# A complex linear recurrence moved from TensorE's cumulative sums to VectorE's scans, and the whole kernel issued in a hand-made order

## The chip, the cores and the metric

The kernel runs on one core of a Trainium2 chip. The metric is the device time of the launch in microseconds (us). Before the change it is 260.15 us (median of 4 runs, 259.61 to 260.87).

The engines are named as in the profile: PE is TensorE (PEld its weight loads), DVE is VectorE, ACT is ScalarE, POOL is GpSimd, SP the queue that issues most DMA transfers. "Span" is the time from the first to the last instruction in the trace; the launch time lies about 2 us above it (260.2 against 258.2 before the change).

## The reference, cut to what matters

Sequence length L = 2048, width 512, 512 complex states, hidden width F = 1792, all in bf16.

```python
xn = layernorm(x)                                    # [1, 2048, 512]
# A: diagonal complex state-space recurrence
Lam_bar = exp(dt * Lam)                              # one complex number per state, |Lam_bar| < 1
Bu = xn @ B_bar.T                                    # complex, [2048, 512]
h[t] = Lam_bar * h[t-1] + Bu[t]                      # for t in range(2048)
A = 2 * real(h @ C.T) + xn * Dskip
# B: gated feed-forward
B = (silu(xn @ w1) * (xn @ w3)) @ w2
out = x + A + B
```

The feed-forward is most of the arithmetic. The two schemes differ in how they do the recurrence.

## The kernel before

Time is cut into 16 chunks of 128 steps, with time on the partitions. Inside a chunk the recurrence is a cumulative sum: the inputs are multiplied by `Lam_bar**-t`, summed over time by a matmul with a triangular matrix, the last state of the chunk before is added by a second matmul, and the result is multiplied by `Lam_bar**t`. The states then have time on the partitions and have to be transposed by DMA for the output matmul.

```python
def ssm_chunk(cl, xnT, h_prev):
    ...                                          # bu_re, bu_im: 4 matmuls each, evicted to bu16 by ACT
    ca = bu16 * einv_re_b                        # 128x1024, DVE
    cb = bu16 * einv_im_b
    zp[:, 0, :] = ca[:, 0, :] - cb[:, 1, :]      # 128x512
    zp[:, 1, :] = ca[:, 1, :] + cb[:, 0, :]
    for ri in range(2):
        hp = ps_mm.tile([P, PS], FP32, name="mm_ps")
        nc.tensor.matmul(out=hp, lhsT=u_caus, rhs=zp[:, ri, :], start=True, stop=(h_prev is None))      # L329
        if h_prev is not None:
            nc.tensor.matmul(out=hp, lhsT=sel, rhs=h_prev[:, ri, :], start=False, stop=True)            # L331
    ...                                          # evicted by ACT, the same four DVE operations with e_re_b, e_im_b
    nc.sync.dma_start_transpose(out=hT16, in_=h16.rearrange("p a b -> p (a b)"))
    return h16, hT16

def glu_up(xnT, hgT):
    for f in range(NFT):                         # 14 steps for each of 4 blocks of 512 rows
        ...                                      # g_ps, u_ps: 4 matmuls each
        nc.scalar.activation(out=th16, in_=g_ps, func=ACT.Tanh, scale=0.5)
        nc.scalar.activation(out=u16, in_=u_ps, func=ACT.Copy, scale=0.5)
        nc.vector.scalar_tensor_tensor(out=th16, in0=th16, scalar=1.0, in1=g_ps, op0=ALU.add, op1=ALU.mult)
        nc.vector.tensor_tensor(out=hgT[:, f, :], in0=th16, in1=u16, op=ALU.mult)
```

A scheduler chooses the order of the instructions on each engine. The layer norm's 1/sqrt is a chain of some ten small DVE operations per chunk in the first block, and the normalised rows are transposed by PE (64 matmuls against an identity).

## Time and profile before

| | before |
|---|---|
| time, median | 260.15 us |
| span of the profiled run, granted TensorE clock | 258.2 us, 1.000 |
| busy: PE, DVE, ACT | 88%, 71%, 49% |
| first gate matmul starts | 24.11 us |
| last output matmul ends | 254.6 us |
| PE waits after the first gate matmul, sum in the view of waits | about 4.5 us |

The view of waits lists who waited for whom: total us, number of times, longest. These are the largest PE entries of the kernel before:

```profile
PE y_ps L286 <- DVE rstd_all L258: 21.1, 2, 18.0
PE gu_ps L297 <- ACT u_339 L302: 1.5, 1, 1.5
PE gu_ps L297 <- ACT u_307 L302: 1.5, 1, 1.5
PE gu_ps L297 <- ACT u_355 L302: 0.7, 1, 0.7
```

The first line is the start: PE waits 18.0 us for the first rstd and once more 3.1 us. Everything else is small. The timeline gives the first gate matmuls and the last output matmuls (start, us, engine, line, operation, how many); four matmuls of 512 columns take 1.87 us at the start, and 1.03 from 27.41 us on:

```profile
24.11 1.87 PE L293 MATMUL gu_ps<-xnT,w_sb 128*128 128x512 bf16 x4 [0.69 <-ACT xnT L287]
...
251.43 3.19 PE L362 MATMUL y_ps<-w_sb,hgT 128*128 128x512 bf16 x14
```

The table of busy time by stretch says that PE is the limit from 45 us on (columns: stretch, its length, busy us and instructions of PE, PEld, DVE, ACT, POOL, then granted clock, DMA share, GB/s):

```profile
28.00:45.00 17.00, 13.21 (x89) 7.14 (x89) 13.48 (x36) 16.62 (x27) 0.00 (x0) 1.00 0.72 158
45.00:62.00 17.00, 16.63 (x104) 8.62 (x105) 16.89 (x44) 12.22 (x22) 0.00 (x0) 1.00 0.01 2
...
150.00:200.00 50.00, 49.73 (x224) 22.28 (x228) 33.47 (x70) 23.02 (x40) 0.00 (x0) 1.00 0.13 30
```

From 150 to 200 us PE is busy 49.73 of 50. PE also counts as busy when it works at half pace (the stretch from 24.10 to 27.40 us is 3.29 of 3.30 us busy with 8 gate matmuls, which start 0.41 us apart on average), so the pitch has to be read too: 22 output matmuls take 4.75 us in the timeline, 0.216 us each. The groups that the change removes or replaces (busy us, mean ns of one; the mean of an L329 matmul is 378 ns, longer than the pitch of 216):

```profile
L329 PE MATMUL mm_ps<-zp,u_caus 128*128 128x512 bf16 x32 | 12.1, 378 | 0.4 <-DVE zp L324 0.2
L337 DVE TENSOR_TENSOR ca<-h16s,e_tab 128x1024 bf16<-128x1024 bf16 x16 | 11.1, 691 | 4.8 <-ACT h16s L335 4.5
```

### The profile page before, as it was taken

How to read it: one execution, taken by the hardware profiler on the slowest of the kernel's cores; microseconds unless marked ns; L12 is line 12 of the kernel's file. 1: busy time of each engine (PE TensorE's matmuls, PEld its weight loads, DVE VectorE, ACT ScalarE, POOL GpSimd, SP SyncE). 2: the span in 40 equal slices, each digit the busy share in tenths (PEclk: the TensorE clock that was granted, in tenths of full speed). 3: DMA queues.
4: the chain of work that ended last, by engine and by line, in shares of the span. 5: the costliest groups of instructions: out<-in, count | busy, mean ns of one | idle time of the engine just before them, and what ended most of it. 6: DMA issues, size and time to landing. Idle time of an engine off the chain costs nothing. (4 is left out here: it accounts for less than half of the span.)

```text
span 258.2 us, 3287 instructions
## 1 busy us (share of the span) xinstructions
PE 227.1 (88%) x1096; PEld 104.7 (41%) x1118; DVE 184.4 (71%) x496; ACT 125.4 (49%) x216; POOL 1.6 (1%) x11
## 2 busy tenths in 40 slices
PE   0014976999999999999999999999999999999994
PEld 0012443455434445444444544444444444444441
DVE  1749887999999739999635399996343899984331
ACT  0614899677733108777400477776100677764000
POOL 2000000000000000000000000000000000000000
PEclk9999999999999999999999999999999999999999
DMA  5999982000122300222201002222010022220000
GB/s 156 155 361 381 349 161 25 1 1 3 23 55 44 83 22 20 41 43 41 42 20 42 22 0 41 42 43 41 0 41 23 20 41 41 43 44 0 20 34 27
DMA packets 33873, 16.73 MB, mean 65 GB/s; under 512 B 23360, under 2 KB 33856, under 8 KB 33856
## 3 DMA queue, kind: packets, MB, share of 16 engines
q1 hardware_dynamic: 31696, 16.00, 23.7%
q10 hardware_dynamic: 2160, 0.53, 2.0%
q8 instruction: 8, 0.13, 0.2%
q14 instruction: 9, 0.07, 0.1%
HBM read 9.18 MB, written 2.10 MB: 44 GB/s over the span
## 5 line engine op out<-in xcount | busy, mean ns | idle before, releaser
L297 PE MATMUL gu_ps<-xnT,w_sb 128*128 128x512 bf16 x222 | 59.4, 382 | 4.1 <-ACT u_339 L302 1.5
L293 PE MATMUL gu_ps<-xnT,w_sb 128*128 128x512 bf16 x218 | 58.5, 383 | 0.9 <-ACT xnT L287 0.7
L362 PE MATMUL y_ps<-w_sb,hgT 128*128 128x512 bf16 x218 | 50.8, 379 | 0.3
L297 PEld LDWEIGHTS <-w_sb 128*128 128x128 bf16 x224 | 21.9, 98 | 31.4 <-issue 9.1
L293 PEld LDWEIGHTS <-w_sb 128*128 128x128 bf16 x224 | 22.1, 99 | 27.5 <-issue 2.1
L362 PEld LDWEIGHTS <-hgT 128*128 128x128 bf16 x224 | 21.9, 98 | 26.4
L287 ACT ACTIVATE xnT<-y_ps 128x512 bf16<-128x512 bf16 x16 | 8.6, 604 | 41.2 <-PE y_ps L286 41.2
L314 PE MATMUL mm_ps<-bbar_im,xnT 128*128 128x512 bf16 x64 | 16.4, 379 | 0.1
L286 PE MATMUL y_ps<-ident,xn_170 128*128 128x128 bf16 x4 | 0.6, 308 | 18.0 <-DVE rstd_all L258 18.0
L310 PE MATMUL mm_ps<-bbar_re,xnT 128*128 128x512 bf16 x61 | 16.3, 378 | 0.1
L337 DVE TENSOR_TENSOR ca<-h16s,e_tab 128x1024 bf16<-128x1024 bf16 x16 | 11.1, 691 | 4.8 <-ACT h16s L335 4.5
L334 ACT ACTIVATE h16s<-mm_ps 128x512 bf16<-128x512 f32 x16 | 9.5, 596 | 9.8 <-PE mm_ps L331 9.4
L329 PE MATMUL mm_ps<-zp,u_caus 128*128 128x512 bf16 x32 | 12.1, 378 | 0.4 <-DVE zp L324 0.2
L339 DVE TENSOR_TENSOR cb<-h16s,e_tab 128x1024 bf16<-128x1024 bf16 x16 | 10.9, 684 | 0.0
L268 DVE BATCH_NORM_STATS2 stats<-x_blk 128x6 f32<-128x512 bf16 x12 | 8.0, 674 | 3.6 <-DMA x_blk<-in_A_x_dram 3.6
L317 ACT ACTIVATE bu_2120<-mm_ps 128x512 bf16<-128x512 f32 x1 | 0.6, 597 | 19.2 <-PE mm_ps L310 19.2
L335 ACT ACTIVATE h16s<-mm_ps 128x512 bf16<-128x512 f32 x16 | 9.5, 595 | 0.0
L314 PEld LDWEIGHTS <-xnT 128*128 128x128 bf16 x64 | 6.3, 98 | 7.6
L310 PEld LDWEIGHTS <-xnT 128*128 128x128 bf16 x64 | 6.1, 97 | 6.6 <-issue 0.7
L286 PEld LDWEIGHTS <-xn_170 128*128 128x128 bf16 x4 | 0.3, 132 | 18.0 <-DVE rstd_all L258 18.0
L324 DVE TENSOR_TENSOR zp<-ca,cb 128x512 bf16<-128x512 bf16 x16 | 6.7, 416 | 0.0
L325 DVE TENSOR_TENSOR zp<-ca,cb 128x512 bf16<-128x512 bf16 x16 | 6.7, 416 | 0.0
(599 smaller groups left out, 364.6 us busy)
## 6 DMA issues: line engine op xcount, KB each, us to landing
w_sb<-in_B_w_dram SPq DMA_DIRECT2D x4, 640.0 KB, 9.6
x_blk<-in_A_x_dram SPq DMA_DIRECT2D x4, 512.0 KB, 8.9
w_sb<-in_B_w_dram SPq DMA_DIRECT2D x1, 1792.0 KB, 12.5
w_sb<-in_B_w_dram SPq DMA_DIRECT2D x2, 512.0 KB, 7.6
b_re_sb<-in_A_B_re_dram SPq DMA_DIRECT2D x1, 512.0 KB, 8.8
b_im_sb<-in_A_B_im_dram SPq DMA_DIRECT2D x1, 512.0 KB, 8.8
ldt_row<-in_A_log_dt_dram ACTq DMA_DIRECT2D x1, 128.0 KB, 6.0
lre_row<-in_A_Lambda_re_dram ACTq DMA_DIRECT2D x1, 128.0 KB, 6.9
```

The costliest lines, as they stand in the source:

```text
L268: nc.vector.bn_stats(out=stats[:, cl, :], in_=xb[:, cl, :])
L287: nc.scalar.activation(out=xnT[:, :, cl * P:(cl + 1) * P], in_=pxt, func=ACT.Copy)
L293: nc.tensor.matmul(out=g_ps, lhsT=w1_sb[:, dt, f * P:(f + 1) * P], rhs=xnT[:, dt, :], start=(dt == 0), stop=(dt == NDT - 1))
L297: nc.tensor.matmul(out=u_ps, lhsT=w3_sb[:, dt, f * P:(f + 1) * P], rhs=xnT[:, dt, :], start=(dt == 0), stop=(dt == NDT - 1))
L310: nc.tensor.matmul(out=bu_re, lhsT=xnT[:, dt, tsl], rhs=bbar_re[:, dt, :], start=(dt == 0), stop=(dt == NDT - 1))
L314: nc.tensor.matmul(out=bu_im, lhsT=xnT[:, dt, tsl], rhs=bbar_im[:, dt, :], start=(dt == 0), stop=(dt == NDT - 1))
L329: nc.tensor.matmul(out=hp, lhsT=u_caus, rhs=zp[:, ri, :], start=True, stop=(h_prev is None))
L334: nc.scalar.activation(out=h16s[:, 0, :], in_=h_ps[0], func=ACT.Copy)
L335: nc.scalar.activation(out=h16s[:, 1, :], in_=h_ps[1], func=ACT.Copy)
L337: nc.vector.tensor_tensor(out=ca2, in0=h16s, in1=e_re_b, op=ALU.mult)
L339: nc.vector.tensor_tensor(out=cb2, in0=h16s, in1=e_im_b, op=ALU.mult)
L362: nc.tensor.matmul(out=y_ps, lhsT=hgT[:, f, tsl], rhs=w2_sb[:, f, :], start=(k == 0), stop=(k == nmm - 1))
```

## The change

The intent is to take the recurrence off TensorE. The states lie on the partitions and time runs along the free axis. The inputs are rotated by `exp(-i*theta*t)`, which leaves a decay by the real number `rho` per state, so the complex recurrence becomes two real ones; each is one scan instruction on VectorE over 512 steps. The result is rotated back, and it already has the layout that the output matmul needs. The 32 cumulative-sum matmuls, the 30 carry matmuls, 64 small setup matmuls and the 16 DMA transposes of states go. The gate uses one Silu eviction and one bf16 product instead of three steps. Transposes of the normalised rows go to DMA for blocks 1 to 3.

The scheduler is switched off. The program emits everything in a written order; a small helper (`Filler`) keeps a queue of VectorE tasks with costs in us, and each PE step calls `bg.fill(budget)`, which emits as many tasks as the budget pays for. The core of the diff:

```diff
+    ctx.enter_context(tc.manual_schedule())
...
+        def pre(pt):                       # rotate the input of one tile of 128 states
+            ...                            # tiles are made; u is the input, st keeps v and g
+            nc.vector.tensor_tensor(out=p1, in0=u, in1=tabq[:, pt, 0:2, :], op=ALU.mult)
+            nc.vector.tensor_tensor(out=p2, in0=u, in1=tabq[:, pt, 2:3, :].to_broadcast([P, 2, TBLK]), op=ALU.mult)
+            nc.vector.tensor_tensor(out=v, in0=p1, in1=p2[:, ::-1, :], op=ALU.subtract)
+        def scan(pt, ri):
+            init = 0.0 if b == 0 else h_blk[b - 1][:, pt, ri, TBLK - 1:TBLK]
+            nc.vector.tensor_tensor_scan(out=st["g", pt][:, ri, :], data0=rho[:, pt:pt + 1].to_broadcast([P, TBLK]),
+                                         data1=st["v", pt][:, ri, :], initial=init, op0=ALU.mult, op1=ALU.add)
+        def post(pt): ...                  # two products and a difference like pre, into h_blk
+        for pt in range(NPT):
+            bg.add(2.0, lambda pt=pt: pre(pt))
+            bg.add(1.1, lambda pt=pt: scan(pt, 0))
+            bg.add(1.1, lambda pt=pt: scan(pt, 1))
+            bg.add(2.0, lambda pt=pt: post(pt), ("ssm", b))
...
+    def y(b):                              # output stage, 4 groups of 128 rows; y_ps has 2 buffers
+        for cl in range(CPB):
+            ...                            # 22 matmuls into y_ps
+            pend.append((cl, y_ps))
+            bg.fill(4.0)                   # (100.0 behind the very last group)
+            while len(pend) > 1:
+                finish()                   # o = y_ps + residual on DVE: this frees the y_ps buffer
...
+    bg.add(0.2, params_w)                  # block 0: tables, and the layer norm of block 1
+    for i in range(NPT + 1):
+        if i < NPT:
+            bg.add(1.9, lambda pt=i: table_angles(pt))
+        for t in ln1a[i:i + 1]:            # one statistics task of block 1 per state tile
+            bg.add(*t)
+        if i >= 1:
+            bg.add(2.1, lambda pt=i - 1: table_q(pt))
+    for t in ln1b:                         # normalise block 1, transpose it by DMA
+        bg.add(*t, ("ln", 1))
+    ...
+    gate = glu(0); bg.flush(("ln", 1)); gate()
+    ssm_tasks(0); bu(0)
+    ...
+    gate = glu(1); gate(); ssm_tasks(1); res_tasks(1); bu(1)
+    fin = y(0)
```

## The prediction

> **What bounds the kernel now.** TensorE, from its first real matmul to the end. The timeline has the first gate matmul at 24.1 us and the last one ending at 254.65; in the stage table PE is 97 to 99% busy from 45 us on, at full granted clock. The longest PE wait in the waits view is the 18.0 us before the first transpose, then 3.1 us for the second half of the layer norm: VectorE had queued later work (and waits for DMA) between the pieces of the first rstd. From 28 to 45 us PE is only 13.2 of 17 us busy, with ScalarE 16.6 busy. VectorE is 71% busy, ScalarE 49%.
>
> Pitch from the timeline: 22 output matmuls take 4.75 us (0.216 each[...]); a gate/up group of 8 takes 1.77.
>
> **Removed from PE.** 32 causal-sum and 30 carry matmuls: 62 x 0.216 = 13.4 us. 64 setup matmuls of 128 columns at 0.056: 3.6, plus about 1 of waiting among them. 48 of 64 layer-norm transposes (now DMA): 2.7. All of this is on the critical path: about 20 us. The ScalarE-bound patch before 45 us cost about 3.8; part comes back (below).
>
> **Moved earlier.** x block 0 arrives as four 128 KB pieces on two queues instead of 512 KB (first statistics at 5.5 us), rstd is Ln and Exp on ScalarE in strict order, weights start with 256 columns. Sum: data 4, two statistics 1.6, Ln/Exp 0.6, apply and transposes 1.4, twice in part: first gate matmul near 10.5 us, 13.5 earlier. It still runs about 3.5 us at half pace, as the first ones do before (4 in 1.87).
>
> **Added.** VectorE: 16 x (six 128x1024 products at 0.60 pitch + two scans). A scan has no duration in this trace[...]. That is 5.8 per state tile, 93 us in all; gates fall from 0.94 to 0.34 (56x: 19), norm 18, residual 9, outputs 10, tables 16: 165 us. Per gate/up step VectorE has about 1.55 us against PE's 1.77, so it keeps up, with little slack.
>
> **New PE time.** 56 steps x 1.77 = 99, 128 input matmuls 27.7, 352 output matmuls 76: 203. Start 10.5 + 203 + half-pace 1.7 = 215, + stalls: ScalarE in block 0 (28 evictions and 12 table sines fill about as long as PE's 24.5) and xnT of block 1, which waits for tables and four DMA transposes (a 256 KB one took 3.1): together 3; later 1.5. Last addition, output DMA and end 3.6 as now: span 223. Reported time lies 2 us above span before, so 225; some of these overlap, so I say 223.
>
> **Predicted: 223 us, 217 to 233.** Faster by over 2%: 0.97; within 2%: 0.02; slower: 0.01.
>
> **What shows it.** First gate matmul at 9 to 12 us; PE about 97% busy from then, output matmuls still 0.216 pitch; scans near 1.1 us; VectorE 75 to 80% of the span; PE waits in block 0 (ScalarE, xnT of block 1) of 2 to 5 us, few later; no PE wait on hidden states at the output matmuls.
>
> **What would make it wrong.** Scans or the reversed-half subtraction taking twice my estimate: VectorE would exceed 200 us and PE would wait on PSUM buffers, toward 235 to 245. GpSimd's chain of small operations holding ScalarE's first sines, which sit in front of evictions. First weights landing late (640 KB took 9.6 us before). Transposed loads of B late for block 0's input matmuls. [...]

The scan's duration, 1.1 us, goes into the forecast of VectorE's work. That sum came to 165 us and contains it: 16 x (6 x 0.60 + 2 x 1.1) is the 93, of which the 32 scans are 35, and the 1.55 us per gate/up step rests on it too. No trace showed a scan before the change, so the 1.1 is the author's estimate with no measurement behind it. The sum of the time, 10.5 + 203 + 1.7 + 3 + 1.5 + 3.6 = 223, contains no scan; 2 was added for the launch and 2 taken off for overlap. The 4 us for the first data is an estimate as well; the first statistics began at 3.4 us after the change.

## The result, and the profile after

The changed kernel takes 237.07 us (median of 4 runs, 236.85 to 237.39). The ratio to before is 0.911 (95% interval 0.909 to 0.913). Ratios here are the mean time of one kernel's runs over that of the other's of the same rounds, so they are not quite the ratio of the medians quoted. It is 23 us faster where 37 were predicted, and 4 us above the upper end of the range.

| | before | after |
|---|---|---|
| time, median | 260.15 us | 237.07 us |
| span, granted TensorE clock | 258.2 us, 1.000 | 234.7 us, 0.975 |
| first gate matmul starts | 24.11 us | 10.03 us |
| last output matmul ends | 254.6 us | 230.9 us |
| busy: PE, DVE, ACT | 88%, 71%, 49% | 90%, 74%, 41% |

The start came as predicted, and the tail is about the same as before (3.8 us behind the last output matmul, 3.6 before). What differs lies between. The PE entries of the view of waits, after:

```profile
PE y_ps L201 <- DVE xn L181: 8.2, 2, 6.3
PE y_ps L428 <- DVE o L421: 4.6, 2, 2.6
PE gu_ps L363 <- DMA xnT<-xn: 4.5, 1, 4.5
PE gu_ps L363 <- ACT g_439 L368: 1.0, 1, 1.0
PE gu_ps L363 <- ACT g_259 L368: 0.6, 1, 0.6
PE bu_ps L311 <- ACT u L313: 0.5, 1, 0.5
PE gu_ps L363 <- ACT g_360 L368: 0.3, 1, 0.3
```

The first line is the start (6.3 us instead of 18.0). The next two are new, long waits in the middle of the kernel: two at the output matmuls for the addition `o`, one at the gate matmuls for the transposed block 1. The timeline of PE shows where:

```profile
10.03 3.62 PE L363 MATMUL gu_ps<-xnT,w_sb 128*128 128x256 bf16 x16
...
51.46 10.91 PE L363 MATMUL gu_ps<-xnT,w_sb 128*128 128x512 bf16 x41 [4.52 <-DMA xnT<-xn]
...
96.44 4.87 PE L428 MATMUL y_ps<-w_sb,hgT 128*128 128x512 bf16 x14 [2.56 <-DVE o L421]
...
150.39 4.87 PE L428 MATMUL y_ps<-w_sb,hgT 128*128 128x512 bf16 x13 [2.04 <-DVE o L421]
```

Undisturbed, 14 output matmuls take 3.19 us; the groups after the two waits take 4.87 (one matmul record of the second is missing). The clock column of the table by stage explains it. The stages are, in order: gate/up of block 0; input matmuls of block 0 and the wait; gate/up of block 1; input matmuls of block 1, undisturbed; output of block 0; gate/up of block 2, undisturbed; output of block 1; output of block 2, undisturbed.

```profile
10.03:39.20 29.17, 27.20 (x130) 13.52 (x131) 19.60 (x46) 22.65 (x45) 6.83 (x26) 1.00 0.63 173
39.20:51.46 12.26, 7.17 (x33) 3.06 (x32) 11.91 (x25) 6.41 (x12) 1.35 (x2) 1.00 0.22 43
51.46:77.31 25.85, 25.75 (x110) 11.32 (x113) 19.79 (x34) 16.12 (x27) 0.00 (x0) 0.93 0.37 87
77.31:84.22 6.91, 6.86 (x32) 3.14 (x32) 5.91 (x8) 4.78 (x8) 0.00 (x0) 1.00 0.00 0
84.22:107.62 23.40, 20.74 (x88) 9.03 (x88) 19.83 (x32) 0.60 (x1) 1.26 (x2) 0.93 0.16 40
107.62:131.79 24.17, 24.07 (x111) 10.98 (x112) 22.30 (x38) 16.12 (x27) 0.00 (x0) 1.00 0.02 7
...
138.70:161.57 22.87, 20.78 (x88) 9.02 (x88) 20.72 (x28) 0.60 (x1) 0.00 (x0) 0.93 0.12 32
...
192.69:211.76 19.07, 18.96 (x87) 8.61 (x88) 11.15 (x15) 0.60 (x1) 0.00 (x0) 1.00 0.06 21
```

After each of the three waits the granted clock is at half for one stretch of 3.413 us (the clock records of the trace: from 52.3, 96.7 and 151.3 us). Half pace for 3.413 us loses 1.71 us. That is the whole excess of gate/up of block 1 (25.85 against 24.17 for block 2). An undisturbed output stage takes 19.0 to 19.1 us, so output 0 lost 4.4 and output 1 lost 3.9: a wait and a half-pace stretch each. In DVE's timeline, the addition that PE waited for stands behind other work:

```profile
89.99 1.38 DVE L181 TENSOR_SCALAR xn<-x_blk,mv_all,rstd_all 128x512 bf16<-128x512 bf16 x4 [1.47 <-POOL rstd_all L210]
91.29 0.68 DVE L325 TENSOR_TENSOR p_1005<-u,tabq 128x1024 bf16<-128x1024 bf16 x1
91.89 0.68 DVE L327 TENSOR_TENSOR p_1007<-u,tabq 128x1024 bf16<-128x1024 bf16 x1
92.61 0.69 DVE L329 TENSOR_TENSOR v<-p_1005,p_1007 128x1024 bf16<-128x1024 bf16 x1
93.34 2.46 DVE L335 TENSOR_TENSOR_SCAN g<-rho,h,v 128x512 bf16<-128x512 f32 x2
95.72 0.67 DVE L421 TENSOR_TENSOR o<-y_ps,xn 128x512 bf16<-128x512 f32 x1
```

The data for `o` were ready near 89 us, when the first 22 output matmuls ended; it ran at 95.72, after the normalisation of block 2 (for which VectorE itself waited 1.47 us for GpSimd's rstd) and a rotation and two scans of block 1, and the third group of matmuls needed the buffer that it frees. The normalisation of block 1 stands at the end of all table work in the same way, and its four transposes then take 5.1 us to issue:

```profile
44.54 1.38 DVE L181 TENSOR_SCALAR xn<-x_blk,mv_all,rstd_all 128x512 bf16<-128x512 bf16 x4
...
44.97 5.12 SPq L216 DMA_TRANSPOSE xnT<-xn  x4
```

The scans, which the profile before could not show (24 with a carry from the block before, 8 without):

```profile
L335 DVE TENSOR_TENSOR_SCAN g<-rho,h,v 128x512 bf16<-128x512 f32 x24 | 30.0, 1274 | 0.2
...
L335 DVE TENSOR_TENSOR_SCAN g<-rho,v 128x512 bf16<-128x512 f32 x8 | 9.5, 1212 | 0.0
```

They take 1.27 and 1.21 us, not the 1.1 estimated. So two explanations compete. Theory: the written order puts work that PE needs soon behind work that it needs late; the waits come from the order, and the half-pace stretches from the waits. Rival: VectorE has more work than the prediction counted, above all in the scans, and any order would make PE wait.

### The profile page after: what moved, and what is told of

Read it like the earlier page. It is cut to its first block, busy times and chain, and to the rows that moved or that the text cites. A ratio compares the mean times of both kernels' runs of the same rounds, so it can differ in the third digit from the quotient of the medians.

```text
span 234.7 us, 2666 instructions
## 1 busy us (share of the span) xinstructions
PE 210.3 (90%) x942; PEld 96.0 (41%) x961; DVE 173.9 (74%) x293; ACT 97.1 (41%) x171; POOL 14.5 (6%) x46
## 4 chain that ended last, share of the span: by engine, by line
PE 62%; DVE 27%; ACT 2%; DMA 2%; issue 2%; POOL 2%; POOLq 0%; SPq 0%; ACTq 0%
PE gu_ps L363 33%; PE y_ps L428 17%; PE y_ps L431 9%; DVE g L335 4%; DVE stats L176 3%; PE bu_ps L311 3%; DVE hgT L375 2%; DVE xn L181 2%; DVE tabq L293 1%; DVE tabq L298 1%; DVE v L329 1%; DVE ang L282 1%; DMA x_blk<-in_A_x_dram 1%; DMA xnT<-xn 1%; DVE mv_all L177 1%
## 5 line engine op out<-in xcount | busy, mean ns | idle before, releaser
L363 PE MATMUL gu_ps<-xnT,w_sb 128*128 128x512 bf16 (+1 forms) x456 | 101.7, 383 | 6.8 <-DMA xnT<-xn 4.5
L313 ACT ACTIVATE u<-bu_ps 128x512 bf16<-128x512 f32 x32 | 19.0, 597 | 31.1 <-PE bu_ps L311 31.1
L421 DVE TENSOR_TENSOR o<-y_ps,xn 128x512 bf16<-128x512 f32 x16 | 11.0, 685 | 27.5 <-PE y_ps L431 24.2
L335 DVE TENSOR_TENSOR_SCAN g<-rho,h,v 128x512 bf16<-128x512 f32 x24 | 30.0, 1274 | 0.2
L431 PEld LDWEIGHTS <-h 128*128 128x128 bf16 x128 | 12.5, 98 | 15.1
L311 PE MATMUL bu_ps<-xnT,bt_re 128*128 128x512 bf16 x62 | 16.2, 379 | 0.6 <-ACT u L313 0.5
L431 PE MATMUL y_ps<-ct_re,h 128*128 128x512 bf16 x63 | 16.4, 379 | 0.1
L311 PE MATMUL bu_ps<-xnT,bt_im 128*128 128x512 bf16 x62 | 16.3, 379 | 0.2
L431 PE MATMUL y_ps<-ct_im,h 128*128 128x512 bf16 x63 | 16.2, 379 | 0.0
L335 DVE TENSOR_TENSOR_SCAN g<-rho,v 128x512 bf16<-128x512 f32 x8 | 9.5, 1212 | 0.0
```

The costliest lines, as they stand in the source:

```text
L311: nc.tensor.matmul(out=ps, lhsT=bt[:, dt, pt * P:(pt + 1) * P], rhs=xnT_blk[b][:, dt, :], start=(dt == 0), stop=(dt == NDT - 1))
L313: nc.scalar.activation(out=u[:, ri, :], in_=ps, func=ACT.Copy)
L335: nc.vector.tensor_tensor_scan(out=st["g", pt][:, ri, :], data0=rho[:, pt:pt + 1].to_broadcast([P, TBLK]), data1=st["v", pt][:, ri, :], in ...
L363: nc.tensor.matmul(out=ps[:, tsl], lhsT=w[:, dt, f * P:(f + 1) * P], rhs=xnT[:, dt, tsl], start=(dt == 0), stop=(dt == NDT - 1))
L421: nc.vector.tensor_tensor(out=o, in0=y_ps, in1=xn_blk[b][:, cl, :], op=ALU.add)
L431: nc.tensor.matmul(out=y_ps, lhsT=h_blk[b][:, pt, ri, tsl], rhs=ct[:, pt, :], start=False, stop=(ri == 1 and pt == NPT - 1))
```

## The experiments

All are edits of the changed kernel; e10 to e13 start from e8_gap_and_first, which is itself such an edit. "After" means 237.07 us and a span of 234.7.

### e1_add_first: the addition ahead of the filled-in tasks

```diff
             pend.append((cl, y_ps))
+            while len(pend) > 1:
+                finish()
             ... bg.fill(4.0)
-            while len(pend) > 1:
-                finish()
```

> Only change: in the output stage the addition that frees the PSUM buffer of row group n goes ahead of the VectorE tasks filled in during row group n+1, instead of behind them. My theory (queue order): the PE waits of 2.56 us (block 0) and 2.04 us (block 1) at the output matmuls go, and with them the two half-pace windows that follow (1.71 us each): span about 8 us shorter, 237 to about 229. Rival (VectorE is simply overloaded, 1.23 us scans instead of the 1.1 I took): the same work has to be done, so the wait moves to the gate/up stage behind it and less than 2 us is gained.

Measured: 228.51 us, correct. Both waits at the output matmuls are gone from the view of waits, and nothing took their place there:

```profile
PE y_ps L201 <- DVE xn L181: 8.4, 2, 6.5
PE gu_ps L363 <- DMA xnT<-xn: 4.5, 1, 4.5
PE gu_ps L363 <- ACT g L368: 2.3, 3, 1.1
PE bu_ps L311 <- ACT u L313: 0.5, 1, 0.5
```

VectorE did the same work (busy 173.1 us, 173.9 after), and its 1.47 us wait for GpSimd is still there, without cost to PE. The order was the cause of these waits; the rival, that any order would make PE wait here, is out. The half-pace stretch after the remaining wait was twice 3.413 us long here (6.83 us), so it is not always 3.413.

### e2_norm1_early: the normalisation of block 1 ahead of most table work

```diff
-        for t in ln1a[i:i + 1]:
+        for t in (ln1a[0:2], ln1a[2:5], ln1b, [], [])[i]:
             bg.add(*t)
         if i >= 1:
-            bg.add(2.1, lambda pt=i - 1: table_q(pt))
+            bg.add(2.1, lambda pt=i - 1: table_q(pt), ("ln", 1))
-    for t in ln1b:
-        bg.add(*t, ("ln", 1))
```

> Only change: VectorE statistics and normalisation of block 1 come before the table work of state tiles 1 to 3 instead of behind all of it. My theory (queue order): the 4.5 us PE wait for the transposed block 1 goes, with its half-pace window: about 6 us shorter, 231. Rival (the four DMA transposes, 1.28 us each to issue, or the DMA queue behind the weights, set the time): the wait stays above 3 us and less than 2 us is gained.

Measured: 230.66 us, correct. The 4.5 us wait is gone. Another took part of its place, because the sines of the last state tile, which came later now, stand before the evictions of the input matmuls in ScalarE's queue:

```profile
42.71 1.02 PE L311 MATMUL bu_ps<-xnT,bt_re 128*128 128x512 bf16 x4 [3.23 <-ACT u L313]
```

No half-pace stretch followed this one, and of the two output waits, which were as before, only the first was followed by one. So 6.4 us came from the wait being 1.3 us shorter and two half-pace stretches fewer (3.4), with the rest in gate/up of block 0, where the input matmuls began 1.6 us earlier.

### e3_keep_warm: useless matmuls in the waits

```diff
+    def warm(n):
+        ps = ps_bu.tile([P, TBLK], FP32, name="bu_ps")
+        for i in range(n):
+            nc.tensor.matmul(out=ps, lhsT=bt_re[:, 0, 0:P], rhs=bt_im[:, 0, :], start=(i == 0), stop=(i == n - 1))
...
+            if cl == 2 and b < 2:
+                warm(8)                     # in y(b)
+    warm(18)                                # after bu(0)
```

> Adds useless matmuls (18 after the input matmuls of block 0, 8 in each of the output stages of blocks 0 and 1) that fill most of the three PE waits; nothing else moves. Theory: the three half-pace windows of 3.4 us are only a consequence of the waits, so clock mean goes from 0.975 to about 0.99 and the time falls by about 5 us (3 x 1.71) although PE does 34 matmuls more. Rival (the pace is granted for another reason, such as power or time): the windows stay and the time is the same or longer.

Measured: 232.10 us, correct; granted clock 0.998, no half-pace stretch between 13.7 and 228.8 us. PE did 34 matmuls more and the kernel became 5.0 us shorter, as three times 1.71 says. The half pace was a consequence of PE standing still, and it is a separate 5.1 us of the loss.

### e4_cheap_scan: scans replaced by cheap products (wrong result)

```diff
-            nc.vector.tensor_tensor_scan(out=st["g", pt][:, ri, :], data0=rho[...], data1=st["v", pt][:, ri, :], ...)
+            nc.vector.tensor_tensor(out=st["g", pt][:, ri, :], in0=tabe[:, pt, 0, :], in1=st["v", pt][:, ri, :], op=ALU.mult)
```

> Wrong result on purpose: each scan is replaced by one 128x512 bf16 product (about 0.34 us instead of 1.23), same order and same consumers, without the carry from the block before. Measures what the scans cost in time. If my mis-sized scan is the main cause, the y waits go with their half-pace windows and more: 8 us or more. In any case the 4.5 us wait for block 1 should stay, since it comes ahead of the first scan. If scans do not matter (order alone), less than 3 us.

Measured: 228.36 us; the result is wrong. VectorE is busy 148.7 us instead of 173.9. The output waits go and the wait for block 1 stays at 4.5 us. The time is that of e1_add_first. So shortening the work in front of the addition helps as much as moving the addition past it, and not more. By the threshold written beforehand (8 us or more) this run alone would have passed for a proof that the mis-sized scan was the main cause; it took e1_add_first to tell the two apart. The product that stands in for a scan takes 0.42 us, far less than the 1.1 predicted, so the run does not say what the mis-sizing alone was worth.

### e6_scheduler: the hand-made order given up

```diff
-    ctx.enter_context(tc.manual_schedule())
```

> The changed kernel with the hand-made order given up: the one line that switches the scheduler off is removed, all instructions are the same. If the hand-made order is a real part of the gain, this is slower than 237 (I guess 240 to 250), with other waits on PE. If the order as written is what hurts, as the first runs suggest in two places, the scheduler could do as well or better (230 to 237).

Measured: 235.70 us, correct, 1.4 us better than the written order. The scheduler normalised block 1 early (no wait for it is listed), began the gate matmuls 1.7 us later (11.73), and had 6.2 us in eight waits of the gate matmuls for ScalarE's evictions. It kept a wait of the same kind at the output matmuls:

```profile
95.83 3.18 PE L427 MATMUL y_ps<-w_sb,hgT 128*128 128x512 bf16 x14 [3.07 <-DVE o L420]
```

So the hand-made order, as written, was no part of the gain.

### e8_gap_and_first: both causes mended

```diff
     ln1a, ln1b = ln_tasks(1)
+    for t in ln1a[0:4]:                    # statistics of block 1 at once, in DVE's idle stretch
+        t[1]()
+    bg.add(*ln1a[4])
     bg.add(0.2, params_w)
     for i in range(NPT + 1): ...
-        for t in ln1a[i:i + 1]:
+        for t in (ln1b if i == 0 else []): # normalise right behind the first angles
             bg.add(*t)
         if i >= 1:
-            bg.add(2.1, lambda pt=i - 1: table_q(pt))
+            bg.add(2.1, lambda pt=i - 1: table_q(pt), ("ln", 1))
-    for t in ln1b:
-        bg.add(*t, ("ln", 1))
```

and the addition first, as in e1_add_first.

> Both causes mended: additions first as in e1_add_first, and the statistics of block 1 in VectorE's idle stretch from 9.5 to 17.5 us, its normalisation right behind the first angles. The theory that the three waits and their half-pace windows are the whole of the miss gives the predicted time: the waits of 4.5, 2.6 and 2.0 us and three windows of 1.7 us go, span about 234.7 - 14 = 221, time about 222 to 224. If something else is behind, it stays above 227.

Measured: 220.84 us (5 runs, 220.71 to 220.93), correct; ratio to before 0.848 (0.845 to 0.850). Span 218.6, granted clock 1.000. All PE waits that the view lists:

```profile
PE y_ps L201 <- DVE xn L181: 8.2, 2, 6.3
PE gu_ps L363 <- ACT g L368: 0.7, 1, 0.7
PE bu_ps L311 <- ACT u L313: 0.4, 1, 0.4
```

This is the best version. The three waits and the half-pace stretches were the miss, and slightly more came (1.2 us less in gate/up of block 0, from 29.2 to 28.0, probably because VectorE has less to do there; that was not tried alone).

### e10_best_cheap_scan: the same with cheap scans (wrong result)

The edit of e4_cheap_scan on e8_gap_and_first.

> Wrong result on purpose: e8_gap_and_first with each scan replaced by one 128x512 product, as in e4_cheap_scan. If the true scan cost matters only through the queue order, this gains less than 1 us over e8_gap_and_first, though VectorE does about 25 us less. If VectorE's total load is a limit of its own, it gains 3 us or more.

Measured: 220.44 us, span 218.6, the same as with real scans to 0.4 us, though VectorE is busy 148.8 us instead of 172.8. Once the order is right, 24 us of scan time cost 0.4 us at most: VectorE's total load is not what sets the time.

### e11_gpsimd_neg: some table work on GpSimd

```diff
-        nc.scalar.activation(out=tabe[:, pt, 2, :], in_=ang, func=ACT.Sin, scale=TWO_PI)
+        gp.tensor_scalar(out=tabe[:, pt, 2, :], in0=tabe[:, pt, 1, :], scalar1=-1.0, scalar2=None, op0=ALU.mult)
...
-        nc.vector.tensor_scalar(out=tabq[:, pt, 1, :], ...)
+        gp.tensor_scalar(out=tabq[:, pt, 1, :], ...)
```

> e8_gap_and_first with one of three table sines per state tile (ScalarE, 0.6 us) and one negation (VectorE, 0.3 us) done on GpSimd instead. ScalarE is what PE waits for in block 0 (2.3 us in three waits for evictions, 0.5 for an input copy): 1 to 2 us shorter than e8_gap_and_first if that holds; no change or longer [...].

Measured: 222.03 us, correct, 1.2 us longer than e8_gap_and_first. A miss. ScalarE is relieved, but one negation takes GpSimd 1.5 to 2.0 us (0.29 on VectorE, 4 of them in the trace after):

```profile
26.28 1.54 POOL L287 TENSOR_SCALAR tabe<-tabe 128x512 bf16<-128x512 bf16 x1 [0.75 <-ACT tabe L286]
27.79 2.02 POOL L295 TENSOR_SCALAR tabq<-tabq 128x512 bf16<-128x512 bf16 x1
```

The wait of the input matmuls for ScalarE grew from 0.4 to 1.2 us. Why the time grew by 1.2 and not by that 0.8 was not followed further.

### e12_pe_back: the removed matmuls put back as useless ones

```diff
+                for dt in range(2):         # before each group of 4 input matmuls, into the same buffer, overwritten
+                    nc.tensor.matmul(out=ps, lhsT=bt[:, dt, 0:P], rhs=xnT_blk[b][:, dt, :], start=True, stop=True)
```

> e8_gap_and_first with 64 useless 128x512 matmuls put back at the input matmuls, as many (62) as the cumulative-sum scheme had at this place. If taking them out of TensorE was worth its full pitch, the time is 64 x 0.216 = 13.8 us longer: 220.8 to 234.5. If VectorE had become the limit, part of it would be hidden: less than 10 us.

Measured: 233.78 us, correct, 12.9 us longer for 64 matmuls, 0.20 us each against a pitch of 0.216. TensorE time at this place counts at nearly its full pitch, as predicted. That the removed cumulative-sum and carry matmuls counted as much in the kernel before is inferred from PE being busy there for 49.73 of 50 us; it was not tried in that kernel.

### e13_one_load: the first x block in one transfer

```diff
-    for c in range(CPB):
-        eng = nc.sync if c < 2 else nc.scalar
-        eng.dma_start(out=x_blk[0][:, c, :], in_=xv[:, c, :])
+    nc.sync.dma_start(out=x_blk[0], in_=xv[:, 0:CPB, :])
```

> e8_gap_and_first with x block 0 fetched in one transfer of 512 KB as before the change, instead of four on two queues. The first statistics began at 5.5 us so before and at 3.4 us after; if the split is what brought that, the first gate matmul moves from 10.1 to about 12 us and the time is 2 us longer. If the rest of the 14 us came from the strict order of the first normalisation, no more than that is lost.

Measured: 220.91 us, correct, 0.07 us longer than e8_gap_and_first: no difference. The first of my two alternatives, 2 us longer, did not come. The first statistics begin 0.9 us later and the gate matmuls 0.8 us later:

```profile
4.33 0.69 DVE L174 BATCH_NORM_STATS2 stats<-x_blk 128x6 f32<-128x512 bf16 x1 [4.33 <-DMA x_blk<-in_A_x_dram]
...
10.94 3.17 PE L361 MATMUL gu_ps<-xnT,w_sb 128*128 128x256 bf16 x16
```

and most of that was made up behind: the first sixteen matmuls run in 3.17 us instead of 3.62, and 0.2 us is left in the span. Of the 14 us by which the first gate matmul moved forward, splitting the transfer brought less than one. The rest is put down to the undisturbed chain of the first layer norm; that was read from the two traces and not tried alone in the kernel before.

## Why the prediction was wrong

**Right.** TensorE bounds the kernel; matmuls put back cost nearly their pitch (e12_pe_back); the first gate matmul starts at 10.03 us (10.5 predicted); VectorE's share is 74%, just under the 75 to 80 predicted. Undisturbed output matmuls kept the pitch of 0.216 us. The predicted sum without stalls was even 2.5 us too long: a gate/up step takes 1.726 us in the changed kernel (24.17 for 14), not 1.77.

**The step that failed** is the sum's term of stalls: "together 3; later 1.5", with "few later". It was 4.5 us for everything; the trace has this instead, each from the stage table:

- Block 0: 8.7 us instead of 3 (29.17 against 24.17 plus the 1.7 entered for the half pace at the start, and 12.26 against 6.91; the 256-column matmuls start 0.21 us apart until 14.74 and 0.11 apart from 14.87 on). The prediction named block 1's normalisation "which waits for tables and four DMA transposes", but entered 3 us for it and ScalarE together, about the 3.1 that it quotes for one transpose; the four took 5.1 us to issue alone, and the last landed 2.45 us after its issue. e2_norm1_early and e8_gap_and_first removed this wait by order alone.
- Output stages: 4.9 us of waits (4.4 and 3.9 less a half-pace stretch each) instead of 1.5. The prediction compared VectorE and PE per gate/up step, and never looked at the output stage, where one group's addition is placed behind a 4 us budget of the next block's work. With the same budget and the addition in front of it these waits are gone: e1_add_first shows it.
- Half pace after the waits: 5.1 us (3 x 1.71), entered as 0. The text named it last among the risks, without a number. e3_keep_warm shows it as 5.0 us.

Together (8.7 - 3) + (4.9 - 1.5) + 5.1 is 14.2 us. The shorter gate/up steps give back 2.5, the earlier start 0.5; and 2 us had been taken off the prediction for overlap that there was not. That makes 13.2 of the 13.7 us between the predicted span of 221 and the measured 234.7.

**Also wrong, with effect only through the order.** A scan takes 1.27 us, not 1.1, and operations that need the result just before them start about 0.12 us later than others (from 91.29 us on, the second product starts 0.60 us behind the first, the difference that needs it 0.72 behind it, the scan that needs the difference 0.73 behind that). A state tile costs about 6.5 us, not 5.8. "Scans taking twice my estimate" was listed as the first danger; e10_best_cheap_scan shows that their length matters only where the order lets it. How much of the 4.9 us of output waits scans of 1.1 us would have left in the written order was not tried.

**Not tried by an experiment: which waits bring half pace.** Their length does not decide it. Waits of 4.52, 2.56 and 2.04 us did (and one of 2.19 us near the start of e6_scheduler), waits of 3.23 (e2_norm1_early) and 3.07 (e6_scheduler) did not, and the same wait of 2.04 us did not in e2_norm1_early. The traces separate the cases in another way. Within each trace the full-pace time between two changes of the clock is a whole number of pieces of 3.413 us (68 before the change; 11, 12, 15 and 23 after it). Cut into these pieces, the matmul records show PE busy for at most 0.39 of the piece just before each half-pace stretch (19 pieces, 12 of them at the end of a kernel), and for at least 0.41 of each of the other 724. In the trace after, the three pieces before the waits' stretches were busy for 0.25, 0.25 and 0.39, the one before the stretch at the end for 0.32, and the lowest of the others for 0.42. So, in these traces, what counts of a wait is how much it takes out of one such piece: the 2.04 us wait left 0.39 of its piece busy after the change, and 0.42 in e2_norm1_early. This was computed afterwards from the twelve traces; no run moved a wait to test it, and the two figures lie close together.

## What to carry to other kernels

On an engine that takes its work in the written order, as VectorE did here (the addition whose data were ready near 89 us ran at 95.72), the total load says little: look at each place where another engine needs its result within a few us, and count the work that stands in front of that instruction. An operation that only frees a buffer deserves the front place (8.6 us in e1_add_first). And when TensorE's waits are estimated, a possible half-pace stretch (1.7 us here for each) belongs to each of them as a term, since three waits of 9 us together cost 14.
